# Moving the turns of three parameter rows forward in TensorE's order

## The chip, the cores and the metric

The kernel runs on one core of a Trainium2 chip. The metric is the device time of one execution in microseconds (us); 182.14 us is the median of three runs of the kernel before (182.12 to 182.43).

## The reference

The input `A_x` is 2048 tokens by D = 448, in bfloat16. It is normalised over its last axis, and the normalised `xn` feeds two branches:

```
xn = layernorm(x)
dt      = exp(log_dt);  Lam = Lambda_re + 1j*Lambda_im
Lam_bar = exp(dt*Lam);  B_bar = ((Lam_bar - 1)/Lam)[:, None] * (B_re + 1j*B_im)
h[t]    = Lam_bar * h[t-1] + xn[t] @ B_bar.T            # 2048 steps, 448 complex states
s       = 2*real(h @ (C_re + 1j*C_im).T) + xn*Dskip
g       = silu((sigmoid(xn @ w_gate) * (xn @ w_up)) @ w_down)   # inner size 1792
out     = x + s*g
```

`log_dt`, `Lambda_im` and `Lambda_re` are vectors of 448. The change is about how these three reach the form in which the kernel uses them.

## The kernel before

The tokens are worked in four chunks of 512 (`TC`), the inner size 1792 in 14 tiles of 128 (`ft`). For each chunk TensorE makes the gate and up products (`g_ps`, `u_ps`), the products with B (`bu`), the down products (`d_ps`) and the products with C (`y_ps`); VectorE runs the recurrence as scans, ScalarE empties PSUM and computes the activations. `keep_order` ties every engine's instructions to the order in which they are written, so nothing is reordered: what is written earlier on an engine runs earlier on it, and an instruction that waits holds all that is written behind it on its engine.

The opening of the kernel, which the change touches, runs like this.

- **The rows.** `load_row` (L144) issues one DMA for each of the three vectors from ScalarE's queue, into the three partitions of the tile `rows`. They are issued in the order `log_dt`, `Lambda_im`, `Lambda_re`, beside the first tokens of x on SyncE's queue (L146, L147, L151).
- **The warming products.** `warm(n, t)` (L202 to L204) issues `n` products of 128x128 by 128x128 into `warm_ps`, whose result nobody reads. With `ones` the operand is a constant; without, it is the identity `ident`, which GpSimd makes at the start.
- **The turns of the rows.** `turn_twice` (L206 to L211) transposes the row tile on TensorE: five small products with 3 rows, four of 128 columns and one of 64, into the PSUM tile `tp_v`. They need all three row DMAs and `ident`.
- **What reads the turns.** `emit_vecs` (L320) copies `tp_v` to `vec` on ScalarE; `emit_dt` (L325) makes dt from it, and GpSimd makes the angles (L330 on).
- **The first tokens.** VectorE takes mean and variance of token tile 0 (`ln_stats`, L220 and L221), ScalarE makes the reciprocal root (`ln_inv`, L253 and L254), VectorE normalises (`ln_norm`, L276), TensorE transposes the result in four products (`ln_turn`, L290, into `tp_x`), and ScalarE copies the transposed pieces to `xnT` (L964). Tile 1 follows in the same way, with two warming products between the transposes of tile 0 and those of tile 1. Only then can the first gate product (`firsts`, L714) be made, which needs `xnT` and the first weights `wg`.

In TensorE's order this stands as: 28 warming products with `ones`; five turns of the rows; 5 warming products with `ident`; 4 transposes of token tile 0; 2 warming products; 4 transposes of token tile 1; the first gate and up products. On ScalarE the order is: `ln_inv(0)`, `emit_vecs`, `ln_inv(1)`, `emit_dt`, then the four copies of L964.

Of the kernel before, what the change touches and what calls it, by code (L numbers as in the profile page):

```python
# [72 lines left out]
def kernel(  # L73
# [126 lines left out]
    ones = nc.const_aps.tensor(1.0, [P, P], BF16)  # L200

    def warm(n, t=ident):  # L202
        for _ in range(n):
            pe.matmul(warm_ps[:], lhsT=t[:, 0:P], rhs=t[:, 0:P], start=True, stop=True)  # L204

    def turn_twice(o, src, n):  # L206

        for kt in range(3):
            pe.transpose(o[:, kt, 0:n], src[:, kt * P:(kt + 1) * P], ident[0:n, 0:n])
        pe.transpose(o[:, 3, 0:n], src[:, D - P:D], ident[0:n, 0:n])  # L210
        pe.transpose(o[0:64, 3, 0:n], src[:, 384:D], ident[0:n, 0:n])  # L211
# [292 lines left out]
    def bank(name, n=TC):  # L504
        return ps.tile([P, n], FP32, name=name, tag="bank", bufs=8)
# [414 lines left out]
    def ln_plan(c):  # L920
# [14 lines left out]
        for j in range(TPC):  # L935
# [3 lines left out]
    dummy = w.tile([P, 1], FP32, name="dummy")  # L939
    act.add_instruction(mybir.InstLoadActFuncSet(name=nc.get_next_instruction_name(), act_func_set_id=LN_AND_EXP,  # L940
                                                 ins=[], outs=[]))
    warm(28, ones)
    turn_twice(tp_v, rows, 3)
    tps = [ps.tile([P, KT, P], BF16, name="tp_x", tag="bank", bufs=8) for _ in range(2)]
    gus = [(bank("g_ps"), bank("u_ps")) for _ in range(3)]
    warm(5)

    ln_stats(0)
    ln_inv(0)
# [258 lines left out]
```

## Time and profile before

| what | value |
|---|---|
| median of three runs | 182.14 us (182.12 to 182.43) |
| the profiled execution's own time | 181.62 us |
| its span, first to last instruction | 179.8 us |
| PE busy | 175.6 us (98%), 1672 products |
| DVE busy | 164.4 us (91%) |
| ACT busy | 114.8 us (64%) |
| POOL busy | 21.6 us (12%) |
| mean granted TensorE clock, from the list of cores | 0.998 |

PE is TensorE's products, PEld its weight loads, DVE is VectorE, ACT ScalarE, POOL GpSimd and SP SyncE; a q behind an engine's name is its queue, where DMAs are issued. The time of an execution holds about 1.8 us outside the span. The ends of products are modelled, so the distance from one product's start to the next (the pitch) tells more of TensorE's pace than the duration of one.

### The profile page before, as it was taken

What the parts mean: (1) busy time and instruction counts of PE and PEld (TensorE: products, weight loads), DVE (VectorE), ACT (ScalarE), POOL (GpSimd) and SP (SyncE); (2) the same over time, 40 slices, a digit from 0 to 9 for tenths busy, and PEclk for the clock granted to TensorE, in tenths of its full rate; (3) what the DMA queues carried; (4) which work ended last, traced back from release to release, by engine and by line L of the source; (5) the groups of instructions that cost most, each with busy time, mean ns of one, the idle gap of its engine ahead of it and who ended that gap; (6) DMA issues with size and microseconds to landing.
All of it is one profiled execution on the core that took longest, in us unless ns stands there. A gap on an engine that the chain in (4) does not pass through costs nothing.

```text
span 179.8 us, 4401 instructions
## 1 busy us (share of the span) xinstructions
PE 175.6 (98%) x1672; PEld 99.9 (56%) x1672; DVE 164.4 (91%) x331; ACT 114.8 (64%) x240; POOL 21.6 (12%) x52
## 2 busy tenths in 40 slices
PE   8999999999999999999999999999999999999992
PEld 7875555556655555555655555555565555645551
DVE  4879999999999789899999999699999989999883
ACT  4999979978398887979177576057048577054100
POOL 3605449331000000014000000000000000000000
PEclk9999999999999999999999999999999999999999
DMA  5999974993343005031600020030001100011011
GB/s 140 315 254 159 292 162 75 338 261 84 80 98 84 18 0 131 4 106 24 91 7 4 0 58 4 0 102 4 0 0 35 29 0 5 0 58 49 0 45 57
DMA packets 26364, 14.27 MB, mean 79 GB/s; under 512 B 16099, under 2 KB 26086, under 8 KB 26342
## 3 DMA queue, kind: packets, MB, share of 16 engines
q1 hardware_dynamic: 26064, 13.72, 30.7%
q8 instruction: 13, 0.21, 0.5%
q10 hardware_dynamic: 278, 0.26, 0.5%
q14 instruction: 9, 0.07, 0.2%
HBM read 7.69 MB, written 1.84 MB: 53 GB/s over the span
## 4 chain that ended last, share of the span: by engine, by line
PE 97%; DVE 1%; ACT 0%; issue 0%; DVEq 0%
PE g_ps L518 25%; PE u_ps L518 20%; PE d_ps L518 18%; PE bu L518 12%; PE y_ps L518 11%; PE d_ps L1151 6%; PE warm_ps L204 2%; PE g_ps L714 1%; PE u_ps L714 1%; PE g_ps L710 1%; PE tp_x L290 0%; DVE sg L864 0%; DVE o_l L870 0%; DVE xn L276 0%; ACT lnv L253 0%
## 5 line engine op out<-in xcount | busy, mean ns | idle before, releaser
L518 PE MATMUL u_ps<-xnT,wu 64*128 64x512 bf16 (+1 forms) x336 | 64.3, 370 | 0.0
L518 PE MATMUL g_ps<-xnT,wg 64*128 64x512 bf16 (+1 forms) x336 | 57.3, 370 | 0.0
L753 ACT ACTIVATE sig<-g_ps 128x512 bf16<-128x512 f32 x52 | 29.4, 604 | 28.3 <-PE g_ps L518 27.7
L518 PE MATMUL bu<-xnT,bT 64*128 64x512 bf16 x168 | 37.4, 376 | 0.0
L518 PEld LDWEIGHTS <-wu 64*128 64x128 bf16 x336 | 25.8, 94 | 16.6 <-issue 0.3
L518 PE MATMUL d_ps<-wd,hF 64*128 64x448 bf16 x336 | 32.3, 349 | 0.0
L518 PEld LDWEIGHTS <-wg 64*128 64x128 bf16 x336 | 23.1, 94 | 15.9
L753 ACT CAST ub<-u_ps 128x512 bf16<-128x512 f32 x52 | 29.5, 614 | 0.1
L518 PEld LDWEIGHTS <-hF 64*128 64x128 bf16 x336 | 19.0, 94 | 12.9
L615 DVE TENSOR_TENSOR_SCAN wv<-r_col,st,ta 128x512 bf16<-128x512 f32 x18 | 22.7, 1277 | 0.2
L518 PE MATMUL y_ps<-ct,h 64*128 64x448 bf16 (+2 forms) x203 | 22.2, 343 | 0.0
L750 DVE TENSOR_TENSOR hF<-sig,ub 128x512 bf16<-128x512 bf16 x52 | 21.1, 419 | 0.9 <-ACT ub L753 0.9
L518 PEld LDWEIGHTS <-bT 64*128 64x128 bf16 x168 | 15.8, 94 | 8.4 <-issue 0.2
L518 PE MATMUL g_ps<-xnT,wt 64*128 64x512 bf16 x52 | 19.6, 376 | 0.0
L518 PE MATMUL u_ps<-xnT,wt 64*128 64x512 bf16 x52 | 19.6, 376 | 0.0
L518 PEld LDWEIGHTS <-h 64*128 64x128 bf16 (+1 forms) x203 | 12.9, 95 | 8.6
L596 ACT CAST bus<-bu 128x512 bf16<-128x512 f32 x24 | 14.5, 605 | 1.3 <-PE bu L518 1.3
L777 ACT ACTIVATE sigd<-d_ps 128x448 bf16<-128x448 f32 x12 | 6.6, 554 | 12.1 <-PE d_ps L518 12.1
L518 PEld LDWEIGHTS <-wt 64*128 64x128 bf16 x104 | 9.8, 94 | 5.3
L248 POOL TENSOR_TENSOR rsd<-ve,mhalf 128x2 f32<-128x2 f32 (+1 forms) x4 | 5.8, 1450 | 47.9 <-PE bu L518 39.3
L1151 PE MATMUL d_ps<-wd,hF 128*128 128x448 bf16 x56 | 10.9, 353 | 0.0
L1154 ACT ACTIVATE g_t<-d_ps 128x448 bf16<-128x448 f32 x4 | 2.2, 544 | 10.5 <-PE d_ps L1151 10.5
(151 smaller groups left out, 235.0 us busy)
## 6 DMA issues: line engine op xcount, KB each, us to landing
wd<-in_B_w_down_dram SPq DMA_DIRECT2D x1, 1568.0 KB
out_dram<-o_t SPq DMA_DIRECT2D x6, 224.0 KB, 2.1
x<-in_A_x_dram SPq DMA_DIRECT2D x2, 448.0 KB, 4.1
x<-in_A_x_dram SPq DMA_DIRECT2D x3, 224.0 KB, 3.4
wu<-in_B_w_up_dram SPq DMA_DIRECT2D x2, 256.0 KB
bsw<-bus SPq DMA_DIRECT2D x4, 128.0 KB, 4.1
wsw<-wv SPq DMA_DIRECT2D x8, 64.0 KB, 2.0
c_re<-in_A_C_re_dram SPq DMA_DIRECT2D x1, 392.0 KB, 9.2
```

What stands on the lines that cost most here:

```text
L204: pe.matmul(warm_ps[:], lhsT=t[:, 0:P], rhs=t[:, 0:P], start=True, stop=True)
L248: pool.tensor_tensor(out=rsd[:, t:t + n, :], in0=ve[:, t:t + n, :], in1=mhalf[:, 0:n, :], op=ALU.pow)
L518: m = pe.matmul(self.t[:, n0:n1], lhsT=lhsT, rhs=rhs, start=self.done == 1, stop=self.done == self.n)
L596: empty = [lambda cc=cc: act.copy(out=bus[:, cc, :], in_=pst[cc][:]) for cc in range(2)]
L615: dve.tensor_tensor_scan(out=T["wv"][:, cc, :], data0=rb, data1=T["ta"][:, cc, :], initial=(0.0 if c == 0 else st[pt][:, cc, :]), op0=mul, ...
L710: pe.matmul(t[:, n0:n1], lhsT=wt[p0:p0 + 64, ft * P:(ft + 1) * P], rhs=xnT[c][p0:p0 + 64, kt, n0:n1], start=first, stop=False)
L714: pe.matmul(t[:, n0:n1], lhsT=(wg, wu)[i][:, k, ft * P:(ft + 1) * P], rhs=xnT[c][:, (GATE_K, UP_K)[i][k], n0:n1], start=first, stop=last)
L750: dve.tensor_tensor(out=h[:], in0=sig[:], in1=ub[:], op=ALU.mult)
L753: u.empty = [lambda: act.activation(sig[:], gt[:], ACT.Sigmoid), lambda: act.copy(out=ub[:], in_=ut[:])]
L777: act.activation(sigd[:], ds[j][:], ACT.Sigmoid)
L1151: pe.matmul(ds[j][:], lhsT=hF[c, ft][:, j * P:(j + 1) * P], rhs=wd[:, ft, :], start=ft == 0, stop=ft == FT - 1)
L1154: act.activation(gs[c][:, j, :], ds[j][:], ACT.Silu)
```

## The change

The turns of the rows stand behind 13 warming products instead of 28. Behind the turns come 18 warming products with `ones`, in one run and before the PSUM tiles of the next stage are taken; the 5 warming products with `ident` that stood there are gone. Ahead of the first transposes there are now 13 + 18 = 31 warming products instead of 28 + 5 = 33. No other engine's instructions are changed or moved.

```diff
-    warm(28, ones)
+    warm(13, ones)
     turn_twice(tp_v, rows, 3)
+    warm(18, ones)
     tps = [ps.tile([P, KT, P], BF16, name="tp_x", tag="bank", bufs=8) for _ in range(2)]
     gus = [(bank("g_ps"), bank("u_ps")) for _ in range(3)]
-    warm(5)
 
     ln_stats(0)
     ln_inv(0)
```

## The prediction

> **What bounds the kernel now.** I read the page's chain of waits first. Its share by engine:
>
> ```profile
> PE 97%; DVE 1%; ACT 0%; issue 0%; DVEq 0%
> ```
>
> TensorE carries the end of the kernel almost alone: from the first products on it hardly stops, so an opening that ends later by some time ends the kernel later by about as much. The page's second part says the same: PE shows 9 in nearly every slice.
>
> So the question is when TensorE comes out of its opening. I read the timeline of the first 10 us (columns: start us, length us, engine, line, operation, out<-in, count, and in brackets the idle time before it with what ended it):
>
> ```profile
> 0.72 0.53 ACTq L144 DMA_DIRECT2D rows<-in_A_log_dt_dram  x1
> 0.76 3.15 PE L204 MATMUL warm_ps<-const-bfloat16-1.0 128*128 128x128 bf16 x28 [0.76 <-PEq L1192]
> ...
> 1.28 0.22 ACTq L144 DMA_DIRECT2D rows<-in_A_Lambda_im_dram  x1
> ...
> 1.53 0.27 ACTq L144 DMA_DIRECT2D rows<-in_A_Lambda_re_dram  x1
> ...
> 3.83 0.15 PEld L209 LDWEIGHTS <-rows 3*128 3x128 bf16 x3 [0.20 <-issue]
> 3.84 0.24 PE L209 MATMUL tp_v<-ident,rows 3*128 3x3 bf16 x3
> ...
> 3.98 0.20 ACT L254 ACTIVATE rsd<-lnv 128x1 f32<-128x1 f32 x1
> ...
> 4.17 0.18 DVE L221 BATCH_NORM_AGGREGATE mv<-stats 128x2 f32<-128x6 f32 x1
> 4.17 0.71 PE L204 MATMUL warm_ps<-ident 128*128 128x128 bf16 x5
> ...
> 4.27 0.37 DVE L276 TENSOR_SCALAR xn<-x,mv,rsd 128x448 bf16<-128x448 bf16 x1
> 4.28 0.17 ACT L320 CAST vec<-tp_v 128x12 f32<-128x12 bf16 x1
> 4.38 0.29 ACT L253 ACTIVATE lnv<-mv,epsb 128x1 f32<-128x1 f32 x1
> ...
> 4.69 0.55 PE L290 MATMUL tp_x<-ident,xn 128*128 128x128 bf16 x4
> ...
> 5.28 1.21 ACT L964 COPY xnT<-tp_x 128x256 bf16<-128x256 bf16 x4 [0.27 <-PE tp_x L290]
> ```
>
> Four things are to be seen. The last row is only issued at 1.53. The turns run at 3.84, yet `vec` starts at 4.28, 0.09 us behind `rsd`: they are hardly late. The transposes of token tile 0 start at 4.69, when `xn` (4.27 + 0.37) is ready and the warming products have just ended: two things end there together. And ScalarE idles 0.27 us for these transposes before its first copy at 5.28; behind that copy stands the first gate product at 5.70.
>
> Two facts come from single records of the same trace. The three rows signal their landing at 1.98, 2.59 and 3.09, and TensorE's wait instruction for the last two is passed at 3.12. And the starts of products are 106.5 ns apart up to 5.00 and 55 to 56 ns apart from 5.08; the clock records put the grant of the full clock at 5.03, 4.27 us behind the first product.
>
> **The part that is moved: turns after 13 products.** Thirteen products start from 0.76 at a pitch of 106.5 ns and leave TensorE free at 2.1. The turns wait for rows that land at 3.09, whatever TensorE does: nothing in the DMA queues is moved. So a pause of about 1.0 us appears from 2.1 to 3.1, where before the rows landed under the 28 products. Queued behind the waiting turns are all of TensorE's instructions. From a landing to a weight load the trace shows 42 ns (`xn` signalled at 4.644, load at 4.686) where the wait sits on the load; here a separate wait instruction of 51 ns comes between, so the first turn is at 3.20. The 0.20 us of idle ahead of the turns is gone into the pause.
>
> **What the earlier turns bring: nothing.** They end 0.64 us earlier, and `vec` can start at 4.19, when `rsd` ends. Behind it on ScalarE stands `lnv` of tile 1 at 4.38, which needs the `mv` of 4.17 + 0.18 = 4.35 and stays there. GpSimd's angles hang on `dt_b` (4.82), which is behind that `lnv`. Gain 0.
>
> **What the 18 products cost.** From the first turn (3.84) to the next warming product (4.17) it is 0.34 us; so the run of 18 starts at 3.54. At the slow pitch it takes 0.08 (the first gap of the run of 5) + 17 x 0.1065 = 1.89 us and ends at 5.43; at the quick pitch 18 x 0.056 = 1.0 us, ending at 4.54. The transposes of tile 0 could start at 4.69, so they start between 0 and 0.74 us late. These are the bounds, and between them the moment of the grant decides. I take the grant at 5.03 as in the trace of before. Then 15 products start by 5.01, the last three at 5.08, 5.14 and 5.19, and the transposes start at 5.25 (before 4.69, +0.56). They are quick now: last start 5.42, signal 0.23 later (as 5.580 to 5.812 for tile 1) at 5.65, against 5.254 before. The first copy goes from 5.28 to 5.67, **+0.39 us**. The first gate product follows at 6.09 instead of 5.70; the transposes of tile 1 end at 5.81 and signal at 5.98, ahead of the third copy at 5.67 + 0.56 = 6.23, so they hide. ScalarE's copies, the `rsd` of tiles 2 and 3 behind them, and TensorE all move by the same 0.39.
>
> **Whether it is given back.** Between 5.70 and 20 us the products of before have small waits of 0.06 to 0.13 us, which end on ScalarE and VectorE; these move along in the case above and give nothing back. I find no wait of TensorE for a DMA there that would absorb a shift. Two warming products fewer are already counted.
>
> **Sum.** 181.62 + 0.39 = 182.01 us for the profiled execution. The median of the runs shown stands 0.52 above that execution, so 182.14 + 0.39 = 182.53, taken as 182.5.
>
> **The clock, weighed against the trace.** The grant came 4.27 us after the first product, over a stretch that held a pause of 0.2 us and the small turns. [...] No row tells how much may be empty. [...]
>
> **Rivals.**
>
> *The pause costs the grant.* If activity must start anew behind the pause, 4.27 us from 3.20 give 7.47. Then the 18 products end at 5.43, tile 0 is signalled at 6.0, TensorE is through with tile 1 at 6.51, and the 18 gate products go at 0.107 us up to 7.47 (9 of them) and at 0.056 after it, ending at 7.97 against 6.76 before: +1.21 us, 183.35. If all 18 are slow, they end at 6.51 + 18 x 0.107 = 8.43: +1.68, 183.8. For it speaks that the only grant in the trace came over a nearly unbroken stretch; against it, that this stretch was not quite unbroken either. [...]
>
> *No delay.* If in the timed runs the grant comes by 3.9, the 18 products end by 4.69 and nothing is late: 182.14. Or the rows land earlier: the run of 18 would have to start by 2.80 even at the slow pitch, so the last row would have to land by 2.35, 0.8 us after its issue starts; the trace has 1.56 and, for the first row, 1.26. So only the first way counts.
>
> *Faster.* The timed runs stand 0.52 us above the profiled one. If that is a later grant (1 us of slow clock behind 5.4 costs about 0.5 us), brought about by the break at 3.6 to 4.2 in before, then the unbroken run of 18 could bring the grant early, and the opening would be as quick as the profiled one at best: 182.14 - 0.52 = 181.6, or 182.0 with the 0.39 on it. It decides only if a break late in the opening harms the grant more than a longer one early. Against it: the profiled execution had its grant at 5.03 in spite of the break.
>
> **How the numbers follow.** Delay by the 18 products with the grant near 5.03: 0.52. Pause costs the grant: 0.30. No delay: 0.10. Faster: 0.08. The bound of what can be told from no change is 0.2%, 0.36 us. The forecast's own range is 0 to 0.74 us, 182.1 to 182.9; its 0.39 is close to the bound, so of its 0.52 I give 0.34 to slower, 0.16 to the same, 0.02 to faster. With the second case all slower, the third 0.08 same and 0.02 faster, the last faster: slower 0.64, same 0.24, faster 0.12. The range runs from 181.9 to 183.9, which leaves out most of the last case and the tails.
>
> **What would show it.** Right: in the timeline of the changed kernel the 13 products end by 2.3, PEld idles about 1 us before L209, the turns start near 3.2, tile 0's transposes (L290) between 4.9 and 5.5 with `xn` long done, the first L964 copy near 5.67, the first L714 product near 6.1, and everything behind it shifted alike. Second case: products still 0.107 us apart beyond 5.5. Wrong: the turns start before 2.8, or TensorE's first product is late and the end is not.

## The result, and the profile after

The changed kernel takes 183.11 us (median of 21 runs, 182.48 to 183.91) against 182.0 us for the kernel before on the same chip (21 runs). The ratio is 1.0058, with a 95% interval of 1.004 to 1.0075: slower by 0.7 to 1.4 us. The profiled execution took 183.34 us with a span of 181.6; it is 1.72 us above the profiled execution of before.

The page's chain of waits, by engine, now has a part that is no engine's work:

```profile
PE 96%; DMA 1%; DVE 1%; ACTq 0%; issue 0%; DVEq 0%
```

The opening in the timeline of TensorE in the changed kernel (columns as in the prediction):

```profile
0.76 1.55 PE L204 MATMUL warm_ps<-const-bfloat16-1.0 128*128 128x128 bf16 x13 [0.76 <-PEq L1192]
3.32 0.22 PE L209 MATMUL tp_v<-ident,rows 3*128 3x3 bf16 x3 [1.01 <-DMA rows<-in_A_Lambda_re_dram]
...
3.64 2.10 PE L204 MATMUL warm_ps<-const-bfloat16-1.0 128*128 128x128 bf16 x18
5.53 0.63 PE L290 MATMUL tp_x<-ident,xn 128*128 128x128 bf16 x4
...
6.62 2.01 PE L714 MATMUL g_ps<-xnT,wg 128*128 128x128 bf16 x18
8.47 0.82 PE L714 MATMUL u_ps<-xnT,wu 128*128 128x256 bf16 x6
```

TensorE waits 1.01 us for the last row. The transposes of tile 0 start at 5.53 instead of 4.69, and the first gate product at 6.62 instead of 5.70. Then comes what the forecast's main case did not have: the 18 gate products need 1.85 us (6.62 to 8.47), where before they needed 1.06 (5.70 to 6.76), as the timeline of the kernel before has it:

```profile
5.70 1.22 PE L714 MATMUL g_ps<-xnT,wg 128*128 128x128 bf16 x18
6.76 0.82 PE L714 MATMUL u_ps<-xnT,wu 128*128 128x256 bf16 x6
```

The groups of instructions between 5 and 10 us show it as the duration of one (last column ahead of the second bar, mean ns); first the kernel before, then the changed one:

```profile
L714 PE MATMUL g_ps<-xnT,wg 128*128 128x128 bf16 x18 | 1.2, 218 | 0.0
```

```profile
L714 PE MATMUL g_ps<-xnT,wg 128*128 128x128 bf16 x18 | 2.0, 306 | 0.0
```

The clock records of the trace say why (each has the start, the length and the granted share): the full clock is granted at 5.03 us in the profiled execution of before and at 8.41 in that of the changed kernel, just as the 18 products end; from the second on they start 0.107 us apart. The mean granted clock does not tell this: it is 0.998 before and 1.000 in the changed kernel, because the records begin with the grant and the slow opening is not in the mean. The u products that follow cross at the quick pace (8.47 to 9.13, as 6.76 to 7.41 before). From there on both kernels do the same work at the same pace, 1.72 us apart.

On ScalarE the earlier turns bring nothing, as the wait ahead of its first copy shows in the timeline of the changed kernel:

```profile
4.16 0.15 ACT L320 CAST vec<-tp_v 128x12 f32<-128x12 bf16 x1
...
4.46 0.30 ACT L253 ACTIVATE lnv<-mv,epsb 128x1 f32<-128x1 f32 x1
...
6.20 1.29 ACT L964 COPY xnT<-tp_x 128x256 bf16<-128x256 bf16 x4 [1.12 <-PE tp_x L290]
```

`vec` is 0.12 us earlier, the `lnv` behind it is not, and the idle time ahead of the copies grew from 0.27 to 1.12 us.

### The profile page after: what moved, and what is told of

The parts are those of the page before. It is cut to its first block, busy times and chain, and to the rows that moved or that the text cites. A ratio compares the mean times of both kernels' runs of the same rounds, so it can differ in the third digit from the quotient of the medians.

```text
span 181.6 us, 4397 instructions
## 1 busy us (share of the span) xinstructions
PE 176.4 (97%) x1670; PEld 101.0 (56%) x1670; DVE 164.5 (91%) x331; ACT 114.8 (63%) x240; POOL 19.9 (11%) x52
## 4 chain that ended last, share of the span: by engine, by line
PE 96%; DMA 1%; DVE 1%; ACTq 0%; issue 0%; DVEq 0%
PE g_ps L518 25%; PE u_ps L518 20%; PE d_ps L518 18%; PE bu L518 12%; PE y_ps L518 11%; PE d_ps L1151 6%; PE warm_ps L204 1%; PE g_ps L714 1%; DMA rows<-in_A_Lambda_re_dram 1%; PE tp_x L290 1%; PE u_ps L714 1%; PE g_ps L710 1%; DVE sg L864 0%; ACTq L144 0%; DVE o_l L870 0%
## 5 line engine op out<-in xcount | busy, mean ns | idle before, releaser
L248 POOL TENSOR_TENSOR rsd<-ve,mhalf 128x2 f32<-128x2 f32 (+1 forms) x4 | 4.9, 1216 | 47.9 <-PE bu L518 39.3
```

What stands on the lines that cost most here:

```text
L248: pool.tensor_tensor(out=rsd[:, t:t + n, :], in0=ve[:, t:t + n, :], in1=mhalf[:, 0:n, :], op=ALU.pow)
```

## The experiments

The question is how the loss divides between two things: the pause of 1 us ahead of the turns, which may cost the grant of the clock, and the second run of 18 products, which ends too late. All seven kernels differ from the changed one in two numbers at most, the products ahead of the turns and behind them. Medians are of 12 executions each; the kernel before, run beside them on the same chip, had 181.91 us (first four) and 182.0 (last three). The ratios and their intervals are not ratios of the two medians, and where the executions of a kernel scatter widely the two differ.

**The pause without the long second run.**

```diff
-    warm(18, ones)
+    warm(10, ones)
```

> 13 products, turns, 10 products: the pause ahead of the turns stays, but the second run ends near 4.7 us, when the first tokens are ready, so it delays nothing. Theory (the pause costs the grant of the full clock): the transposes of tile 0 start near 4.7 as in the kernel before, yet the products stay 0.107 us apart until a grant behind 6 us, and the time is about 0.7 us above the kernel before (0.4 to 1.1), near 182.7. Rival (the 18 products themselves are the cost): within 0.2 us of the kernel before.

Measured: 182.76 us, ratio to the kernel before 1.0045 (1.0021 to 1.0069). TensorE's timeline of this run:

```profile
4.78 0.63 PE L290 MATMUL tp_x<-ident,xn 128*128 128x128 bf16 x4
...
5.88 2.10 PE L714 MATMUL g_ps<-xnT,wg 128*128 128x128 bf16 x18
7.77 1.49 PE L714 MATMUL u_ps<-xnT,wu 128*128 128x256 bf16 x6
```

The first tokens are transposed 0.09 us later than before, the first gate product starts 0.18 later, and still the u products only start at 7.77 (before 6.76) and are slow themselves (1.49 us for six, before 0.82). The grant came at 9.28. So the pause alone costs 0.85 us of median (0.4 to 1.3 by the interval); the rival falls.

**The long second run without the pause.**

```diff
-    warm(13, ones)
+    warm(23, ones)
```

> 23 products, turns, 18 products: the first run ends when the rows land, so there is hardly a pause, and the second run ends as late as in the changed kernel (transposes of tile 0 near 5.5 if the clock is slow till then). Theory (pause costs the grant): the grant comes before 7.2 us, the time is 0.2 to 0.6 us above the kernel before, near 182.4, well below the changed kernel. Rival (the 18 products are the cost): as slow as the changed kernel, 1.0 us above the kernel before.

Measured: 182.64 us, ratio 1.0033 (1.0008 to 1.0057). The median is 0.73 us above the kernel before, a little over what the theory gave, and the interval reaches to the rival's 1.0. The profile decides more than the time: the grant came at 4.32, the run of 18 ended at the quick pace (1.26 us from its start to that of the transposes, in the changed kernel 1.89), and the transposes of tile 0 started at 5.12.

```profile
3.86 1.42 PE L204 MATMUL warm_ps<-const-bfloat16-1.0 128*128 128x128 bf16 x18
5.12 0.38 PE L290 MATMUL tp_x<-ident,xn 128*128 128x128 bf16 x4
...
5.96 1.22 PE L714 MATMUL g_ps<-xnT,wg 128*128 128x128 bf16 x18
```

That execution took 181.92 us. This is the forecast's main case: the grant in time, and 18 products in the way.

**Nothing ahead of the turns.**

```diff
-    warm(13, ones)
     turn_twice(tp_v, rows, 3)
```

> No products ahead of the turns, then 18: TensorE is idle till the rows land near 3.2 us. [...] Rival (products ahead of the pause count towards the grant, as a sum would): the grant falls about 1 us later than in the changed kernel, and the time is 0.3 to 0.6 us above it, 183.4 to 183.7.

Measured: 182.96 us, ratio 1.0053 (1.0024 to 1.0083), with a grant at 9.14 in its profile. That is the changed kernel's time within 0.15 us. The rival's 183.4 to 183.7 did not come: by the median the 13 products ahead of the pause bring nothing, though in the two profiles the grant is 0.73 us earlier with them (8.41 against 9.14), one execution each.

**Half the pause.**

```diff
-    warm(13, ones)
+    warm(18, ones)
```

> 18 products, turns, 18 products: a pause of about 0.5 us instead of 1.1; the turns and the second run stay where the changed kernel has them. [...]

Measured: 183.0 us, ratio 1.0057 (1.0033 to 1.0081). The wait for the row is 0.6 us instead of 1.0, the grant is at 8.11, and nothing is gained. From the end of the first run (2.63) to the start of the second (3.73) 1.1 us hold nothing but the small turns, and in the profiled execution the grant followed 4.38 us after that start.

**Early turns, no pause, a second run that ends in time.**

```diff
-    warm(13, ones)
+    warm(23, ones)
     turn_twice(tp_v, rows, 3)
-    warm(18, ones)
+    warm(10, ones)
```

> 23 products, turns, 10 products: the turns are as early as the rows allow, with hardly a pause, and the second run ends near 4.8 us, so neither the pause nor the length of the second run is there. Theory (the changed kernel loses by a pause that costs the grant and by 18 products where 10 have room): within 0.2 us of the kernel before, and 0.3 to 0.6 us under the run with 23 and 18 products. Rival (turning early is itself the loss, by another order of reads on ScalarE): as slow as the run with 23 and 18, 0.6 to 0.7 us above the kernel before.

Measured: 182.08 us, ratio 1.0 (0.9973 to 1.0027); grant at 5.30. The turns start at 3.33, as early as in the changed kernel, and nothing is lost:

```profile
3.33 0.22 PE L209 MATMUL tp_v<-ident,rows 3*128 3x3 bf16 x3
...
5.78 1.21 PE L714 MATMUL g_ps<-xnT,wg 128*128 128x128 bf16 x18
```

So it is not the place of the turns that costs, and with both faults out the time is that of the kernel before. Against the run with 23 and 18 the 10 products give 0.56 us back (182.64 to 182.08); the two ran on different chips and their intervals overlap, so this difference is likely and not shown.

**A pause elsewhere.** This one leaves the turns where the kernel before has them and takes away the five products behind them.

```diff
-    warm(13, ones)
+    warm(28, ones)
     turn_twice(tp_v, rows, 3)
-    warm(18, ones)
```

> 28 products, turns where the kernel before has them, and no product behind them: TensorE idles from 4.2 us until the first tokens are ready near 4.7; no useful work is delayed by the edit. [...] Rival (what costs is an early pause, or the late turn of the rows' waiters): within 0.2 us of the kernel before.

Measured: 183.06 us, ratio 1.0038 (1.0008 to 1.0067). Its timeline has every useful step up to the first gate product within 0.12 us of where the kernel before has it:

```profile
3.84 0.23 PE L209 MATMUL tp_v<-ident,rows 3*128 3x3 bf16 x3
...
4.70 0.61 PE L290 MATMUL tp_x<-ident,xn 128*128 128x128 bf16 x4 [0.46 <-DVE xn L276]
...
5.82 2.13 PE L714 MATMUL g_ps<-xnT,wg 128*128 128x128 bf16 x18
```

The 12 executions fall apart: four at 181.71 to 181.89, one at 182.50, seven at 182.93 to 183.69. The profiled one (183.29) has its grant at 9.12. Five products that compute nothing are worth 1.06 us of median, though nothing waits for them; with two groups of executions the median lies in the slower one, and by the ratio it is 0.7 us (0.15 to 1.2).

**A pause of 0.5 us.**

```diff
-    warm(13, ones)
+    warm(20, ones)
     turn_twice(tp_v, rows, 3)
-    warm(18, ones)
+    warm(10, ones)
```

> 20 products, turns, 10 products: a pause of about 0.5 us ahead of the turns, and the second run ends in time. [...]

Measured: 182.17 us, ratio 1.0008 (0.9981 to 1.0035). The wait for the row is 0.4 us here. This pause costs little in most executions: nine of the 12 lie at 182.45 or below, though the interval leaves room for 0.6 us. The profiled execution (182.59) had its grant at 7.49.

**What the profiles say together.** Each run has one profiled execution with a time and a grant:

| products ahead, behind | grant, us | time, us |
|---|---|---|
| 28, 5 (before) | 5.03 | 181.62 |
| 23, 10 | 5.30 | 181.72 |
| 20, 10 | 7.49 | 182.59 |
| 28, 0 | 9.12 | 183.29 |
| 13, 10 | 9.28 | 183.39 |
| 23, 18 | 4.32 | 181.92 |
| 18, 18 | 8.11 | 183.26 |
| 13, 18 (changed) | 8.41 | 183.34 |
| 0, 18 | 9.14 | 183.80 |

In the first five the first tokens are transposed in time (4.68 to 4.81), and the time follows the grant: from 5.30 to 9.28 it grows by 1.67 us over 3.98 us, 0.42 us for each us of late grant, and the two runs between lie within 0.05 us of that line, though in the one with 20 and 10 the first gate products also waited 0.21 us for their weights. The changed kernel at 8.41 would by that line stand at 181.72 + 0.42 x 3.11 = 183.03; it stands at 183.34. So of its 1.72 us about 1.4 are the clock and 0.3 the long second run, by this estimate. The other three with 18 behind do not speak against it: 18, 18 and 0, 18 lie 0.36 and 0.47 above the line, and 23, 18 lies 0.30 above the kernel before. The opening seems to say otherwise, since 0.92 of the 1.72 us lie ahead of the first gate product; but products that are held back until after the grant then follow each other at the quick pace, 0.056 us instead of 0.107, so part of that delay is made up. No run holds the grant fixed to show this by itself. The medians say much the same: 0.85 for the pause (13 and 10), and 183.11 - 182.76 = 0.35 for the eight more products, which is less than the intervals of the two can tell apart.

## Why the prediction was right or wrong

The direction was right (slower, 0.64), 183.11 lies inside 181.9 to 183.9, and the size was not: 0.39 us was forecast and 1.1 measured. The main case alone had 182.1 to 182.9, which leaves 183.11 out; the range holds it because it was drawn to take in the second case. And the larger part of the loss is not the one that the main case forecast: the delay by the 18 products is about 0.3 of the 1.72 us in the profiles, the late grant about 1.4. That 183.11 lies inside is owed to the rival, and that the main case pointed the same way is in part luck.

- **The pause.** Forecast 1.0 us from 2.1 to 3.1, turns at 3.20. Measured 1.01, turns at 3.32; the last row landed 0.1 later in that execution (3.19). Right.
- **Nothing from the earlier turns.** Right: `lnv` of tile 1 did not move forward, and the run with 23 and 10 shows early turns without loss or gain.
- **The second run of 18.** Right as a mechanism; with the grant in time it put tile 0 at 5.12 (forecast 5.25) in the run with 23 and 18. In the changed kernel it went at the slow pitch to its end, and the transposes start at 5.53, the forecast's upper bound of 5.43 plus the later row.
- **The failed step is "I take the grant at 5.03 as in the trace of before".** The grant moved. The rival priced this: with all 18 gate products slow +1.68 us, ending at 8.43. The profiled execution shows +1.72 and an end at 8.47, and the sign named for that case, products still 0.107 us apart beyond 5.5. It had 0.30 of the chance and should have been the likeliest case. The only grant that the trace of before showed came over a stretch that held a pause of 0.2 us and the small turns; no row showed one over a stretch with 1 us empty, so to keep it there was the bolder of the two assumptions. The rival had the effect right and its moment wrong: a fixed 4.27 us from a new start gives 7.47, while from the start of the products behind the pause to the grant the six kernels with a pause show 3.72, 4.38, 4.42, 4.78, 5.32 and 5.54 us.
- **A second fault lies under it: one profiled execution was read as if its grant were fixed.** The nine profiles have it at nine places from 4.32 to 9.28, one for each kernel, so no two grants of the same kernel are on record. That it falls at another place in each execution, and that the median is taken over such places, is an estimate of the author's from the times: with 28 and 0, four executions lie at 181.71 to 181.89 and seven at 182.93 to 183.69. The 0.52 us by which the timed runs stood above the profiled one fits this, and is not shown: the 21 executions of before range from 181.60 to 182.44 but for two (182.94 and 184.06), which at 0.42 us for each us would be a spread of 2.0 us of grant.
- **The rival "faster"** rested on the break at 3.6 to 4.2 in the kernel before. In the profiled execution the grant came at 5.03, behind that break and in spite of it; with 23 and 10 products the break lies half a microsecond earlier and the ratio is 1.0.
- **The rival "no delay"** needed grants by 3.9; none was seen in nine profiles, and the fastest of the changed kernel's 21 executions is 182.48, above the median of before.

That no later wait gives the shift back was right: the 1.72 us of the opening are the 1.72 us of the end.

The experiments point to no version below both kernels. The kernel before already has its grant at 5.03 in its profile and ends its second run when the first tokens are ready; what seems to be left in it is the moment of the grant, and no run here shows a kernel that sets it.

## What to carry to other kernels

In this opening the number of products that only keep TensorE busy was not what counted: what counted is that the stretch they fill has no large hole. With 36 products and a hole of 1.1 us between their two runs (18 and 18) the profile had the grant at 8.11 and the median was 183.0; with 33 and a hole of 0.48 us (23 and 10) these were 5.30 and 182.08. Before an instruction that waits for a DMA is moved forward in the order of an engine, look up when that DMA lands; here the row landed at 3.1 us, and the 13 or 18 products ahead of it ended 1.0 and 0.6 us before the turns could start. And where the start of a kernel runs at a clock that is granted later, read the grant from several executions, since one trace shows one grant only.

## What the runs showed that was not expected

The hole that goes with a late grant can be bracketed in the nine profiles. The hole is counted from the end of the first run of products (its last start plus the pitch of 0.107 us) to the next product that is not a turn of the rows. It was 0.47 us in the kernel before, 0.48 in the run with 23 and 10 and 0.70 with 23 and 18, and the grants came at 5.03, 5.30 and 4.32. It was 0.93 us with 20 and 10, 1.0 with 28 and 0, 1.1 with 18 and 18, 1.5 in the changed kernel and 1.6 with 13 and 10, and the grants came at 7.49, 9.12, 8.11, 8.41 and 9.28; with nothing ahead of the turns (0 and 18) it came at 9.14. Between 0.70 and 0.93 us the point stays open. So does whether the length of the hole alone decides, since each kernel has one profile: the times of the run with 20 and 10, and four of the 12 with 28 and 0, suggest that some of these executions had an earlier grant, but no profile of them shows one.

The other surprise is how little a shorter wait helps down to 0.6 us: cutting it from 1.0 to 0.6 us with the second run kept (13 and 18 to 18 and 18) changed 183.11 to 183.0, and taking all 13 products away changed it to 182.96. With 18 behind and hardly a wait (23 and 18, 0.17 us) it was 182.64. That the step between is sharp is not shown, since the intervals of these runs overlap; with 10 behind, a wait of 0.4 us already left most executions as quick as those of the kernel before.
